# The first modulation's 128 uneven pieces in eight transfers instead of six

## The chip, the cores and the metric

One core of a Trainium2 chip. The metric is the device time of one execution in microseconds (us); a time given for a kernel is the median of its runs. Engines are named as the profile names them: PE is TensorE, DVE VectorE, ACT ScalarE, POOL GpSimd, SP SyncE. SP issues all loads of this kernel; the bytes are moved by the core's 16 DMA engines.

## What is computed

One transformer block for one token, with modulation from a condition vector and with attention over a cache of 8192 positions:

```python
mod = (silu(c) @ w_mod)              # 640 -> 6 x 640: sa, ca, ga, sb, cb, gb
h = layernorm(x) * (1 + ca) + sa
q = (h @ wq)                         # 32 heads of 192
p = softmax(q @ k_cache.T * 192**-0.5)   # per head, 8192 positions
x = x + ga * ((p @ v_cache) @ wo)
h = layernorm(x) * (1 + cb) + sb
x = x + gb * (relu(h @ w1 + b1)**2 @ w2 + b2)
```

All of it is in float32. The keys and values alone are 403 MB, read once.

## The kernel before, in words

All data in memory is laid out so that every load is a plain block of 128 rows. The loads go out on SP's one queue in the order of the program:

- `wm0_t` (L122): the first modulation's weights, the first query weights and the small vectors, 128 rows of 8514 floats.
- `wm0x` (L125): the rest of the first modulation. The last block of rows (`b == KB - 1` in `mod`) is split in a way of its own: 480 of its 1280 columns (`WX`) of each of the 128 rows are a *piece*, 1920 bytes. The 128 pieces are put into 64 rows of at most `SX = 7` pieces, as the table `XP` says: an entry `(a, k, n)` is one transfer of `k` rows, to rows `a`, `a+4`, ... of the tile, with `n` pieces side by side in a row. Pieces that no transfer fills stay at zero, set by two memsets (L120 on DVE for the first 3 pieces of a row, L121 on POOL for the other 4), and add nothing to the sum.
- `chunk0`, `chunk1`, ... (L240, in `load`): 53 blocks of keys, values, query weights and output weights, most of about 8 MB, in a ring of three buffers (`slot`); `wm0_t` lies in the same ring. After them come the loads of the second half (`wm1`, `w1`, `w2`, the last one in four parts).

On the other engines the program begins with `silu`, the product `mod(0, 2, ...)` (L198 for what is laid out evenly, L204 for the pieces: two matmuls for each of the 7 places of a row, whatever lies there), a layernorm, and the first query (L254). From then on DVE multiplies each chunk of keys by its query (L273) and sums (L281), PE sums up the values (L322), and the buffer is given back to `load(n + 3)`.

The framework gives each transfer a semaphore that counts its landing. It has eight for SP's queue (DMAHW0 to DMAHW7), handed out in turn, and a transfer that gets one that was used before is issued only after the transfer that used it has landed. A wait that SP stands at holds everything behind it on SP.

Of the kernel before, what the change touches and what calls it, by code (L numbers as in the profile page):

```python
# [38 lines left out]
EXTRA = {"o": WO, "q": WQ}  # L39
SLOT = 84 * DH  # L40
SX = 7
XP = ((32, 8, 5), (0, 3, SX), (1, 3, SX), (2, 3, SX), (3, 3, 6), (33, 1, SX))
WX = 3 * DG
W0 = KB * 2 * D - WX
VPC = 5
# [48 lines left out]
def block_kernel(ctx: ExitStack, tc: tile.TileContext, kv, wm0, wm0x, wm1, w1, w2, out):  # L94
# [28 lines left out]
    r = 0  # L123
    for a, k, n in XP:
        nc.sync.dma_start(wm0x_t[a:a + 4 * k:4, :n * WX], wm0x[r:r + k, :n * WX])  # L125
# [397 lines left out]
```

## Time and profile before

| | us |
|---|---|
| median of 3 runs | 1052.29 |
| lowest and highest | 1051.96, 1052.34 |
| the profiled execution: span from the first to the last instruction | 1050.0 |
| DVE busy | 826.1 |
| PE busy | 488.7 |

The profiled execution is told by its span; its own time on the device isn't given apart from that, and the median of the runs is 2.29 us over the span. The page gives the busy time of each engine, the DMA engines' busy share and rate in 40 slices, and the chain of work that ended last. The trace behind it can be asked for stretches: what each engine did in order of time, what SP issued and when, and how many bytes began to move in each slice of a stretch.

### The profile page before, as it was taken

The numbers are of one execution on the slowest core, as the hardware profiler recorded it, in microseconds if no ns is written. First come the engines' busy times: TensorE is split into PE (matmuls) and PEld (weight loads), VectorE is DVE, ScalarE is ACT, GpSimd is POOL, SyncE is SP. The second block draws the span as 40 slices with busy tenths as digits, with TensorE's granted clock in tenths as the row PEclk, the third lists the DMA queues.
The fourth block names the chain that finished last, engine by engine and source line by source line (L and its number), as shares of the span: only waits on it lengthen the run. The fifth ranks groups of instructions, "written<-read, shape, count | busy, mean of one in ns | idle before, by whom it ended". The sixth has DMA issues, their size and how long they took to land.

```text
span 1050.0 us, 5180 instructions
## 1 busy us (share of the span) xinstructions
PE 488.7 (47%) x2130; PEld 133.8 (13%) x2130; DVE 826.1 (79%) x405; ACT 44.9 (4%) x122; POOL 190.4 (18%) x61
## 2 busy tenths in 40 slices
PE   3253334455352363446354356345445346435287
PEld 1010001111010010101011011001011011001023
DVE  1799878876959969888697895999887977988812
ACT  0100000000000000000000000000000000000001
POOL 1113121121212211212121121122211211311200
PEclk9676576777685686668776576686777767768689
DMA  9999999999999999999999999999999999999998
GB/s 408 430 433 432 434 435 433 446 439 433 431 432 433 428 433 433 433 442 434 432 434 433 433 434 437 435 433 435 436 430 433 433 435 433 435 433 426 431 429 345
DMA packets 9144, 452.14 MB, mean 431 GB/s; under 512 B 1033, under 2 KB 1037, under 8 KB 1421
## 3 DMA queue, kind: packets, MB, share of 16 engines
q1 hardware_dynamic: 9118, 451.83, 99.5%
q8 instruction: 16, 0.26, 0.1%
q14 instruction: 6, 0.05, 0.0%
q10 hardware_dynamic: 4, 0.00, 0.0%
HBM read 451.82 MB, written 0.00 MB: 430 GB/s over the span
## 4 chain that ended last, share of the span: by engine, by line
DMA 53%; DVE 33%; PE 12%; ACT 1%; issue 0%; SPq 0%; DVEq 0%; ACTq 0%
DMA chunk<-in_kv 50%; DVE chunk L273 17%; DVE sc L281 13%; PE ps_o L322 6%; PE ps_q L254 2%; PE att_a L354 2%; DMA w_t<-in_w 2%; DMA wm_t<-in_wm 1%; DVE os L336 1%; DVE om L334 1%; PE ps_mx L297 1%; PE att_a L356 1%; ACT p L305 0%; PE ps_mod L198 0%; PE ps_mod L204 0%
## 5 line engine op out<-in xcount | busy, mean ns | idle before, releaser
L273 DVE TENSOR_TENSOR chunk<-chunk,qb 128x8064 f32<-128x8064 f32 (+19 forms) x81 | 419.6, 5211 | 127.3 <-DMA chunk<-in_kv 122.1
L281 DVE TENSOR_REDUCE sc<-chunk 128x25 f32<-128x4800 f32 (+21 forms) x109 | 333.8, 3096 | 0.4
L399 POOL TENSOR_TENSOR chunk<-chunk 128x1824 f32<-128x1824 f32 (+9 forms) x51 | 187.3, 3673 | 801.0 <-DVE chunk L273 568.6
L322 PE MATMUL ps_o<-chunk,p 128*32 128x512 f32 x1536 | 288.6, 719 | 70.1 <-DMA chunk<-in_kv 60.6
L297 PE MATMUL ps_mx<-ident,mp 128*128 128x128 f32 x32 | 14.6, 457 | 347.6 <-DVE mp L295 347.5
L322 PEld LDWEIGHTS ps_o<-chunk,p 128*32 128x32 f32 x1536 | 66.2, 129 | 268.1 <-issue 183.2
L354 PE MATMUL att_a<-chunk,oW 128*32 128x512 f32 x96 | 66.5, 850 | 45.0 <-ACT oW L352 45.0
L254 PE MATMUL ps_q<-chunk,ln_h 128*128 128x512 f32 x110 | 64.5, 746 | 25.2 <-DMA chunk<-in_kv 25.2
L297 PEld LDWEIGHTS ps_mx<-ident,mp 128*128 128x128 f32 x32 | 5.7, 177 | 376.3 <-DVE mp L295 308.2
L305 ACT ACTIVATE p<-sc,nm 128x256 f32<-128x256 f32 x32 | 16.2, 507 | 651.0 <-DVE nm L299 651.0
L254 PEld LDWEIGHTS ps_q<-chunk,ln_h 128*128 128x128 f32 x110 | 25.9, 246 | 61.6 <-issue 33.1
L334 DVE TENSOR_TENSOR om<-ps_o,mask 96x512 f32<-96x512 f32 x32 | 21.6, 675 | 8.9 <-PE ps_o L322 8.9
L299 DVE TENSOR_REDUCE nm<-ps_mx 128x1 f32<-128x128 f32 x32 | 9.3, 292 | 19.6 <-PE ps_mx L297 19.6
L354 PEld LDWEIGHTS att_a<-chunk,oW 128*32 128x32 f32 x96 | 12.4, 145 | 82.4 <-ACT oW L352 47.6
L336 DVE TENSOR_REDUCE os<-om 96x64 f32<-96x512 f32 x32 | 21.8, 682 | 1.1
L344 DVE TENSOR_REDUCE oT<-ps_oT 128x3 f32<-128x96 f32 x16 | 4.0, 248 | 18.4 <-PE ps_oT L340 18.4
L310 PE MATMUL ps_sum<-ident,wide 128*128 128x128 f32 x16 | 7.5, 467 | 22.4 <-ACT wide L308 22.4
L340 PE MATMUL ps_oT<-ident,os 96*128 96x96 f32 x16 | 4.9, 306 | 26.9 <-DVE os L336 26.9
L198 PE MATMUL ps_mod<-wm_t,silu 128*32 128x480 f32 (+2 forms) x78 | 9.1, 606 | 14.4 <-DVE silu L180 14.4
L356 PE MATMUL att_a<-chunk,oW 128*96 128x384 f32 x32 | 14.5, 536 | 0.0
L352 ACT ACTIVATE oW<-oT,r 128x96 f32<-128x96 f32 x16 | 5.9, 372 | 173.3 <-DVE oT L344 173.3
L255 ACT ACTIVATE qb<-ps_q 128x512 f32<-128x512 f32 x12 | 7.2, 597 | 130.6 <-PE ps_q L254 130.6
(79 smaller groups left out, 99.8 us busy)
## 6 DMA issues: line engine op xcount, KB each, us to landing
chunk<-in_kv SPq DMA_DIRECT2D x38, 8064.0 KB, 35.3
chunk<-in_kv SPq DMA_DIRECT2D x11, 8000.0 KB, 36.6
chunk<-in_kv SPq DMA_DIRECT2D x2, 7872.0 KB
chunk<-in_kv SPq DMA_DIRECT2D x1, 6144.0 KB, 22.8
wm_t<-in_wm SPq DMA_DIRECT2D x1, 4480.0 KB
wm_t<-in_wm SPq DMA_DIRECT2D x1, 4257.0 KB, 12.5
chunk<-in_kv SPq DMA_DIRECT2D x1, 3264.0 KB
chunk<-in_kv SPq DMA_DIRECT2D x1, 3072.0 KB
```

What stands on the lines that cost most here:

```text
L254: nc.tensor.matmul(ps, h1[:, b:b + 1].to_broadcast([P, P]), w[:, b], start=(b == 0), stop=(b == KB - 1))
L273: nc.vector.tensor_mul(pr, pr, q[:, None, :].to_broadcast([P, b - a, DH]))
L281: nc.vector.tensor_reduce(sc[:, a % SRING:a % SRING + b - a], src[:, a - first:b - first], axis=AX.X, op=ALU.add)
L297: nc.tensor.transpose(ps[:, :P], mp.to_broadcast([P, P]), ident)
L299: nc.vector.tensor_reduce(nm, ps[:, :P], axis=AX.X, op=ALU.max, negate=True)
L305: nc.scalar.activation(p, s[:, :, None].to_broadcast([P, NPOS, 32 // E]), AF.Exp, bias=nm, accum_out=sp[:, h % 2:h % 2 + 1])
L322: nc.tensor.matmul(ps_t[h][32 * g:32 * (g + 1)], p[:, E * j:E * (j + 1)].rearrange("p e r -> p (e r)"), t[:, g], start=(j == 0), stop=last)
L334: nc.vector.tensor_mul(om[:n], ps_t.pop(h)[:n].rearrange("p (d e) -> p d e", e=E), mask[:n, None, :].to_broadcast([n, ED, E]))
L336: nc.vector.tensor_reduce(os_[:n, h % 2], om[:n], axis=AX.X, op=ALU.add)
L354: nc.tensor.matmul(att_a[96:, :512], oW[:, j], w[:, j, :512], start=(first and j == 0), stop=(last and j == NV - 1))
L356: nc.tensor.matmul(att_a[:96, :NV * (D - 512)], oW.rearrange("p j r -> p (j r)"), w[:, :, 512:], start=first, stop=last)
L399: nc.gpsimd.tensor_add(half, half, kt[:, m:, DH // 2:])
```

## The change

Only the table `XP` differs. Before, 21 rows in 6 transfers carry 5, 7, 7, 7, 6 and 7 pieces a row; after, 32 rows in 8 transfers carry 2, 3, 4, 5, 7, 7, 4 and 2. Both carry the same 128 pieces, and the tile, the memsets and the matmuls are the same (the host fills `xp` and `xs` by the same table).

```diff
-XP = ((32, 8, 5), (0, 3, SX), (1, 3, SX), (2, 3, SX), (3, 3, 6), (33, 1, SX))
+XP = ((32, 7, 2), (33, 6, 3), (34, 5, 4), (35, 4, 5), (0, 3, SX), (1, 3, SX), (2, 3, 4), (3, 1, 2))
```

By row of a transfer, the pieces add up so: rows that stand first in their transfers carry 39 pieces before and 34 after; second and third rows 32 before and 32 after; the fourth to eighth 5 each before, and 14, 9, 5, 2 and 0 after.

SP's queue at the start of the program, before. `wm_t` is the tile of the first load and of the pieces, `chunk_100` and the following are chunk 0, 1, 2 and 3; in brackets stands what the issue waits for.

```order
L122 DMA wm_t<-in_wm 128x8514
L125 DMA wm_t<-in_wm0x 8x2400 [waits DVE_49,Pool_49]
L125 DMA wm_t<-in_wm0x 3x3360 x3
L125 DMA wm_t<-in_wm0x 3x2880
L125 DMA wm_t<-in_wm0x 1x3360
L240 DMA chunk_100<-in_kv 128x12288
L240 DMA chunk_102<-in_kv 128x16000 [waits DMAHW0_49]
```

And the same stretch after, where `chunk_102` and the following are chunk 0, 1 and 2:

```order
L122 DMA wm_t<-in_wm 128x8514
L125 DMA wm_t<-in_wm0x 7x960 [waits DVE_49]
L125 DMA wm_t<-in_wm0x 6x1440
L125 DMA wm_t<-in_wm0x 5x1920 [waits Pool_49]
L125 DMA wm_t<-in_wm0x 4x2400
L125 DMA wm_t<-in_wm0x 3x3360 x2
L125 DMA wm_t<-in_wm0x 3x1920
L125 DMA wm_t<-in_wm0x 1x960 [waits DMAHW0_49]
L240 DMA chunk_102<-in_kv 128x12288 [waits DMAHW1_49]
L240 DMA chunk_104<-in_kv 128x16000 [waits DMAHW2_49]
```

The first load uses DMAHW0. Before, the six transfers of pieces use 1 to 6, chunk 0 uses 7, and chunk 1 is the first that waits for a semaphore in use, that of the first load. After, the eighth transfer of pieces is the one that waits for the first load, and chunk 0 stands behind it and waits for the first transfer of pieces.

## Rows read from the trace of the kernel before

**Rows 1.** The page: span, engines, DMA in 40 slices, queues.
```profile
span 1050.0 us, 5180 instructions
PE 488.7 (47%) x2130; PEld 133.8 (13%) x2130; DVE 826.1 (79%) x405; ACT 44.9 (4%) x122; POOL 190.4 (18%) x61
...
DMA  9999999999999999999999999999999999999998
GB/s 408 430 433 432 434 435 433 446 439 433 431 432 433 428 433 433 433 442 434 432 434 433 433 434 437 435 433 435 436 430 433 433 435 433 435 433 426 431 429 345
...
q1 hardware_dynamic: 9118, 451.83, 99.5%
q8 instruction: 16, 0.26, 0.1%
```
**Rows 2.** Chain that ended last, program's end: start us, us, what.
```profile
1027.20 18.48 DMA w_t<-in_w
1045.72 0.75 PE ps_y L464 x16
1046.50 0.52 PE ps_y L464 x8
```
**Rows 3.** The same chain, program's beginning.
```profile
0.73 12.46 DMA wm_t<-in_wm
13.21 0.20 DVE small L129
...
19.05 3.90 PE ps_mod L204 x22
...
34.89 12.97 DVE chunk L273
```
**Rows 4.** SP in order of time: start us, us, engine, line, operation, tiles, count.
```profile
0.73 0.39 SPq L122 DMA_DIRECT2D wm_t<-in_wm  x1
3.28 4.11 SPq L125 DMA_DIRECT2D wm_t<-in_wm0x  x6
7.44 0.35 SPq L240 DMA_DIRECT2D chunk<-in_kv  x1
...
13.21 0.33 SPq L240 DMA_DIRECT2D chunk<-in_kv  x1
```
**Rows 5.** Line L125: issues on SP, ns min/median/max, first and last start.
```profile
L125 SPq DMA_DIRECT2D wm_t<-in_wm0x x6: 411/651/801, 3.3 to 7.0; - x6
```
**Rows 6.** What SP waited for from 0 to 60 us: us, times, longest.
```profile
SPq L240 <- DMA wm_t<-in_wm: 5.4, 1, 5.4
```
**Rows 7.** DMA issues, whole run: count, KB each, median us from issue to landing.
```profile
chunk<-in_kv SPq DMA_DIRECT2D x38, 8064.0 KB, 35.3
...
chunk<-in_kv SPq DMA_DIRECT2D x1, 6144.0 KB, 22.8
...
wm_t<-in_wm SPq DMA_DIRECT2D x1, 4257.0 KB, 12.5
```
**Rows 8.** DMA by slices of 62.5 ns, 0.5 to 3.0 us.
```profile
GB/s 0 0 0 0 0 0 0 0 0 0 0 0 0 0 0 0 0 0 0 2180 545 545 2724 1090 0 1090 545 0 0 0 0 0 0 0 0 0 0 0 0 0
```
**Rows 9.** The same, 12.0 to 14.5 us.
```profile
GB/s 0 0 0 0 0 307 0 461 1727 940 940 1573 1788 2575 786 786 215 0 0 0 215 215 0 0 215 0 0 0 215 215 0 0 215 0 0 0 0 1942 786 786
```
**Rows 10.** The same, 1047.5 to 1049.5 us (50 ns a slice), the output's transfers.
```profile
GB/s 0 0 0 0 0 0 0 0 0 0 0 0 0 0 0 0 0 0 0 0 26 0 26 0 0 0 0 0 0 0 0 0 0 0 0 0 0 0 0 0
```
**Rows 11.** SP in order of time, the output.
```profile
1047.76 0.28 SPq L470 DMA_DIRECT2D out_y<-y  x1
```
**Rows 12.** Stretches: us, busy us of PE, PEld, DVE, ACT, POOL, clock, DMA share, GB/s.
```profile
200.00:300.00 100.00, 45.94 (x181) 12.07 (x180) 81.84 (x38) 3.39 (x10) 17.97 (x5) 0.72 1.00 434
```
**Rows 13.** The same at the end.
```profile
1043.20:1043.60 0.40, 0.40 (x20) 0.34 (x12) 0.00 (x0) 0.00 (x0) 0.00 (x0) 1.00 0.75 308
...
1044.00:1045.00 1.00, 0.79 (x24) 0.68 (x24) 0.00 (x0) 0.00 (x0) 0.00 (x0) 1.00 0.76 315
1045.00:1045.60 0.60, 0.23 (x8) 0.00 (x0) 0.00 (x0) 0.00 (x0) 0.00 (x0) 1.00 0.73 291
1045.60:1046.00 0.40, 0.28 (x8) 0.27 (x12) 0.00 (x0) 0.00 (x0) 0.00 (x0) 1.00 0.51 198
1046.00:1046.50 0.50, 0.48 (x17) 0.15 (x8) 0.00 (x0) 0.00 (x0) 0.00 (x0) 1.00 0.00 0
```
**Rows 14.** DVE in order of time, with idle time before and its releaser.
```profile
59.19 6.15 DVE L273 TENSOR_TENSOR chunk<-chunk,qb 128x5760 f32<-128x5760 f32 x1
...
106.26 9.03 DVE L273 TENSOR_TENSOR chunk<-chunk,qb 128x1920 f32<-128x1920 f32 x2 [1.33 <-DMA chunk<-in_kv]
```

## The prediction

> **What bounds the kernel now.** I read the page first. The 16 DMA engines are 90% busy or more in every one of the 40 slices but the last, at 430 to 440 GB/s, while DVE is busy 79% and PE 47% of the span [rows 1]. So the loads are the bound: 452 MB at about 434 GB/s, the rate of the undisturbed middle [rows 12], are 1042 us of a span of 1050. Next the chain's two ends. At the end the chain is a load, three short products that wait for the last parts of it, and two DVE steps [rows 2]: whatever makes the last landing late makes the kernel late. At the beginning the chain is not on the loads: the first load lands at 13.19 (0.73 + 12.46), then come `silu`, the product, the layernorm and the first query, and DVE takes up chunk 0 only at 34.89 [rows 3]. Chunk 0 has landed by then (issued at 7.44, 22.8 us to landing: about 30.3) [rows 4, 7]. DVE first stands idle for a chunk just before 106.26 [rows 14]. In between it works off a lead that the loads have, and the DMA queue has a chunk or two in hand at all times (35.3 us from issue to landing [rows 7], against 8064 KB at 434 GB/s = 19.0 us). From 13 us to the end the loads thus run without a break, and a break anywhere is not made good later: the rate has no reserve.
>
> That is the question to put to this change: does it open a break in the loads, or does it only move pieces about?
>
> **The pieces.** A piece of 1920 bytes on one of 16 engines that share 434 GB/s (27.1 each) takes 71 ns. The slices after 13 us show single rows of 13.4 KB (215 GB/s in 62.5 ns) starting one after another about half a microsecond apart, while other engines begin the longer rows of chunk 0 [rows 9]. I read this as rows of one transfer going to different engines, and the first three rows of every transfer to the same three. So one engine has 39 pieces before (2.77 us), two have 32 (2.27), five have 5 (0.35), and eight have none. After, that is 34, 32, 32, then 14, 9, 5, 2, 0, and eight with none. Moving them costs no bytes: −0.35 us on the most loaded engine, +0.64 at worst on another. The two added issues on SP take 0.65 us each by the median of the six [rows 5]; the first seven fit between 3.28 and about 8.0, while the first load still moves until about 12.9. They are hidden. The memsets don't change, and the first transfer's shorter wait brings nothing, as DVE's memset is the later one.
>
> **The wait.** The eighth transfer of pieces has the semaphore of the first load, so SP holds it until that load has landed, and chunk 0 stands behind it on SP. Before, chunk 0 goes out at 7.44, and it is chunk 1 that waits there, 5.4 us, and goes out at 13.21, with chunk 0's bytes to cover it [rows 4, 6]. After, at 13.21 only the last small transfer goes out. I take 0.41 us for it: the shortest of the six, since the issues' times (3.28 to 7.39 in all, the last at 7.0) leave that for the one-row transfer [rows 4, 5]. With the gap of 0.05 that stands between the pieces and chunk 0 before, **chunk 0 goes out at 13.67, 6.23 us later**. Its own wait, for the first transfer of pieces, is over by then: that one's bytes are at the head of each engine's line behind the first load. The first load's bytes ran out at about 12.4 to 12.9: the engines begin the next rows there [rows 9]. From then until chunk 0's first bytes come, nothing but pieces is queued.
>
> How long is that break? The one load that starts from idle in this trace is the first: 12.46 us from issue to landing, of which 4257 KB (4.36 MB) at 434 GB/s are 10.04, so 2.42 us are lags at both ends [rows 3, 7]. Chunk 0 after would land at 13.67 + 2.42 + 14.50 (6144 KB at the same rate) = 30.59 on all engines. Before, on an engine without pieces, it follows the first load directly: 13.19 + 14.50 = 27.69. So those eight engines lose **2.90 us**. The five with 5 pieces would have landed 0.35 later anyway and lose **2.55**. Those with 32 pieces lose 0.63, the one with 39 about 0.1: their pieces fill the break. The low bound takes the lag as the output's transfers show it, 0.74 us or so from issue to the first byte (issued at 47.76, bytes from the slice at 48.50) [rows 10, 11]: 13.67 + 0.74 − 12.9 = **1.5 us**. Chunk 0 is a load from memory like the first, whose first bytes come 1.0 us after the issue and not before 1.75 [rows 4, 8], and whose first rows were slow as well, since no further row begins before 3.0; so I take it to be near the first load's lag. The high bound has 0.65 for the small issue and not 0.41: 3.14.
>
> [...]
>
> **Does the break reach the end?** Only if the engines that are last at the end are among those that lose. If only the three with 32 to 39 pieces were late, 13 of 16 would be idle in the last two microseconds. They are not: from 1043.2 to 1045.6 the DMA share is 0.73 to 0.76, which is 12 of 16 engines [rows 13]. So besides the three, nine others are as late at the end, which had 5 pieces or none. The page shows something that falls on single engines: 16 instruction fetches of 16 KB on a queue of their own (0.26 MB) [rows 1]. I take it that an engine which serves one moves nothing else meanwhile. Whatever made the nine late, they were 2.3 us ahead at chunk 0 and are not at the end, and 2.5 to 2.9 us more at the beginning are 2.5 to 2.9 more at the end. As the rows don't say whether one with 5 pieces or with none is the very last, I take the middle, **+2.7 us**. Nothing hides it: the compute at the beginning has 34.89 − 30.59 = 4.3 us left for chunk 0, and later chunks come later for DVE, which waits for them anyway from 106 us on. The pieces themselves are needed at 19.05 [rows 3]; the last would land at about 13.2 + 2.27 + 0.14, well before.
>
> **Sum.** On the profiled execution: 1050.0 + 2.7 = 1052.7. The median of the runs stands 2.29 over that span, so 1052.29 + 2.7 = **1055.0 us**, 0.26% slower.
>
> **Rivals.**
>
> *The loaded engines cover it (not slower).* The end is set by the engines with 39 and 32 pieces, which lie 2.3 to 2.8 us behind the others from the first chunk on. Then the break is spent where the others wait in any case, and what counts is 5 pieces fewer on the most loaded engine less the little it loses: −0.35 to +0.63, 1051.9 to 1052.9. It decides if at most three engines are at work in the last 2 us before the last landing. For it speaks that before the change these engines are the last at chunk 0 by the sum above; against it the 12 of 16. Chance 0.11. [...]
>
> *The break isn't there.* SP's wait ends earlier than I take it to, or the engines hold enough work: the time stays, 1052.3. For it would speak a chunk 0 that is issued before 13.2, and nothing in the order or in the 5.4 us that chunk 1 waits does. Chance 0.03.
>
> *One engine more in the way.* The wait for two more transfers adds instructions on PE and SP; if this brings one more fetch of 16 KB on an engine that is among the last, it loses what a fetch costs, 16 KB at 27.1 GB/s = 0.6 us and, if it has to wait its turn behind a row of 64 KB, up to some 2.4 more: 1055.6 to 1058. Chance 0.06.
>
> **How the numbers follow.** The forecast has 0.80. Its own range is 1052.29 + 1.5 to 1052.29 + 3.14, 1053.8 to 1055.4. I give 1053.8 to 1055.7, since the last rival begins there. Of 0.2% as the least that a measurement of this kernel can tell from no change, the bound is 1054.4, a break of 2.1 us; the low part of the forecast's range is under it, for which I set 0.10 of the 0.80. So slower is 0.70 + 0.06 = 0.76; same is 0.10 + 0.11 + 0.03 = 0.24, of which I give 0.01 to faster, for no case reaches 1050.2.
>
> **What would show it.** In the profile after: SP issues seven transfers of pieces by about 8.0, one at 13.2, and chunk 0 at about 13.7, with the wait for the first load in front of L125 and no longer in front of L240; between 13 and 14.7 us the DMA share falls to three to five engines of 16, with hardly any bytes beginning, and then 16 rows of 48 KB begin within half a microsecond; chunk 0 is about 17 us from issue to landing, not 22.8; the last landing comes 2.7 us later, and the steps behind it are unchanged. The prediction is wrong if chunk 0 goes out before 13, or if the last landing moves by under 2 us though the gap is there: then the late engines at the end are those that had the pieces, or the start from idle is faster than the first load's.

## The result and the profile after

| | before | after |
|---|---|---|
| median of 6 runs, us | 1052.12 (1051.96 to 1052.34) | 1055.34 (1054.80 to 1055.55) |
| profiled execution, span, us | 1050.0 | 1053.0 |

The ratio is 1.003, with a 95% interval of 1.002 to 1.004: the changed kernel is slower by 3.2 us. Forecast were 2.7 us and 1055.0.

The page, where it answers to [rows 1]: the busy times of the engines are nearly as before (PE 6.4 us more), the bytes too. Only the first of the 40 slices moves clearly fewer, 367 GB/s and not 408.

```profile
span 1053.0 us, 5182 instructions
PE 495.1 (47%) x2130; PEld 134.8 (13%) x2130; DVE 826.2 (78%) x405; ACT 44.9 (4%) x122; POOL 190.4 (18%) x61
...
GB/s 367 434 434 431 429 437 439 435 435 434 432 435 434 427 431 437 434 440 433 433 427 434 434 440 433 429 434 436 439 434 432 429 434 439 431 434 424 430 430 339
...
q8 instruction: 17, 0.28, 0.1%
```

SP in order of time after, from 8 to 14 us (start us, us, what; it answers to [rows 4]), and what SP waited for in the first 60 us (it answers to [rows 6]):

```profile
7.77 5.65 SPq L125 DMA_DIRECT2D wm_t<-in_wm0x  x2
13.47 0.82 SPq L240 DMA_DIRECT2D chunk<-in_kv  x2
...
SPq L125 <- DMA wm_t<-in_wm: 4.7, 1, 4.7
```

The seventh transfer of pieces starts at 7.77, the eighth ends at 13.42, and chunk 0 goes out at 13.47, where it was 7.44. The wait for the first load, in front of L240 before, stands in front of L125 now.

The stretch from 13.0 to 14.4 us in the kernel before and after (us, busy us of PE, PEld, DVE, ACT, POOL, clock, DMA share, GB/s begun):

```profile
13.00:14.40 1.40, 0.03 (x4) 0.03 (x5) 0.76 (x4) 0.21 (x1) 0.00 (x0) 1.00 0.36 154
```
```profile
13.00:14.40 1.40, 0.10 (x4) 0.10 (x8) 0.76 (x4) 0.21 (x1) 0.00 (x0) 1.00 0.23 96
```

This table books a row where it begins, so the first line doesn't mean idle engines: before, 13 engines were in the middle of a row of chunk 0 that had begun by 13.0 [rows 9]. After, nothing but pieces begins here, at a share of 0.23, 3.7 engines of 16, where the prediction has three to five. The slices show it better. The bytes that begin to move, in slices of 100 ns, are in the kernel before from 12 to 16 us, and in the changed one from 14 to 18 us:

```profile
GB/s 0 0 0 192 288 1079 1175 1966 1744 983 134 0 0 269 0 134 0 0 269 0 134 0 0 1214 983 1590 1966 1966 0 134 0 0 0 0 492 0 0 0 0 0
```
```profile
GB/s 134 0 0 134 2043 2534 492 530 77 0 0 983 492 492 0 0 0 0 0 0 0 0 0 492 0 0 0 492 0 492 492 2458 492 492 0 492 0 1475 0 492
```

A row of chunk 0 is 49 KB, 492 GB/s in one slice. Before, the first rows begin at 12.5 to 12.9 (what begins at 12.4 are pieces) and the second ones at 14.3 to 14.7: a row takes 1.8 us. After, 15 first rows begin at 14.4 to 15.3 and the 16th at 16.3; the second rows begin at 16.8 to 17.9. So there are two losses: the rows begin some 2 us later, and an engine's first row takes mostly 2.2 to 3.3 us where it took 1.8.

At the program's end the chain is as before [rows 2], with the last wait 3.12 us later (1049.62 against 1046.50):

```profile
1030.68 18.11 DMA w_t<-in_w
1048.84 0.75 PE ps_y L464 x16
1049.62 0.52 PE ps_y L464 x8
```

### The profile page after: what moved, and what is told of

It reads as the page before. It is cut to its first block, busy times and chain, and to the rows that moved or that the text cites. A ratio compares the mean times of both kernels' runs of the same rounds, so it can differ in the third digit from the quotient of the medians.

```text
span 1053.0 us, 5182 instructions
## 1 busy us (share of the span) xinstructions
PE 495.1 (47%) x2130; PEld 134.8 (13%) x2130; DVE 826.2 (78%) x405; ACT 44.9 (4%) x122; POOL 190.4 (18%) x61
## 4 chain that ended last, share of the span: by engine, by line
DMA 56%; DVE 30%; PE 13%; ACT 1%; issue 0%; SPq 0%; DVEq 0%; ACTq 0%
DMA chunk<-in_kv 53%; DVE chunk L273 16%; DVE sc L281 12%; PE ps_o L322 6%; PE ps_q L254 2%; PE att_a L354 2%; DMA w_t<-in_w 2%; DMA wm_t<-in_wm 1%; DVE os L336 1%; DVE om L334 1%; PE att_a L356 0%; PE ps_mod L198 0%; ACT p L305 0%; PE ps_mx L297 0%; PE ps_mod L204 0%
## 5 line engine op out<-in xcount | busy, mean ns | idle before, releaser
L297 PE MATMUL ps_mx<-ident,mp 128*128 128x128 f32 x32 | 14.5, 452 | 348.0 <-DVE mp L295 348.0
L354 PE MATMUL att_a<-chunk,oW 128*32 128x512 f32 x96 | 69.2, 880 | 44.9 <-ACT oW L352 44.9
L354 PEld LDWEIGHTS att_a<-chunk,oW 128*32 128x32 f32 x96 | 12.5, 146 | 82.4 <-ACT oW L352 47.6
L198 PE MATMUL ps_mod<-wm_t,silu 128*32 128x480 f32 (+2 forms) x78 | 9.3, 619 | 14.3 <-DVE silu L180 14.3
```

What stands on the lines that cost most here:

```text
L198: nc.tensor.matmul(ps[32 * g:32 * (g + 1), at], e[:, b:b + 1].to_broadcast([P, 32]), wg, start=(b == 0), stop=(b == KB - 1 and (wx is None ...
L297: nc.tensor.transpose(ps[:, :P], mp.to_broadcast([P, P]), ident)
L354: nc.tensor.matmul(att_a[96:, :512], oW[:, j], w[:, j, :512], start=(first and j == 0), stop=(last and j == NV - 1))
```

## The experiments

The theory: the loss is the time that chunk 0 is issued too late to follow the first load without a break. Its rivals: the pieces' new places on the engines; the number of transfers; the one instruction fetch more that the page shows (17 and not 16). Each time stands beside that of the kernel before on the same chip, 1051.98 to 1052.12.

| kernel | chunk 0 goes out, us | median, us | ratio to before, 95% interval |
|---|---|---|---|
| before | 7.44 | 1052.0 | |
| `pool2`: the changed table, chunk 0 not held | 7.76 | 1052.5 | 1.0005 (0.9996 to 1.0014) |
| `six_even`: six transfers, other places | 7.70 | 1052.1 | 1.0002 (0.9993 to 1.001) |
| `d9`: chunk 0 held by POOL | 9.01 | 1051.97 | 1.0 (0.9991 to 1.0009) |
| `d10`: the same, longer | 10.01 | 1053.45 | 1.0012 (1.0002 to 1.0021) |
| `d12`: the same, longer still | 11.76 | 1053.47 | 1.0012 (1.0004 to 1.0021) |
| `seven`: old places, seven transfers | 13.34 | 1055.07 | 1.0029 (1.0017 to 1.004) |
| after: eight transfers | 13.47 | 1055.34 | 1.003 (1.002 to 1.004) |
| `ten`: old places, ten transfers | 14.43 | 1056.37 | 1.0041 (1.0027 to 1.0055) |
| `filled`: as `seven`, 983 KB more | 13.19 | 1056.15 | 1.0039 (1.0026 to 1.0051) |
| `filled2`: as `seven`, 1966 KB more | 13.27 | 1056.39 | 1.004 (1.0028 to 1.0053) |

### The changed table without the wait

```diff
-    for a, k, n in XP:
-        nc.sync.dma_start(wm0x_t[a:a + 4 * k:4, :n * WX], wm0x[r:r + k, :n * WX])
+    for i, (a, k, n) in enumerate(XP):
+        queue = nc.sync if i < 6 else nc.gpsimd
+        queue.dma_start(wm0x_t[a:a + 4 * k:4, :n * WX], wm0x[r:r + k, :n * WX])
```

> The changed table as it is, eight transfers with 34, 32, 32, 14, 9, 5 and 2 pieces on the engines, but the last two are issued from POOL's queue, which has semaphores of its own. SP then has the first load, six transfers of pieces and chunk 0 on eight semaphores, and chunk 0 waits for nothing. If the break before chunk 0 is the whole loss, the time is that of the kernel before, 1052.1 us within 0.4, and chunk 0 is issued by about 8 us. If the pieces' new places or the number of transfers cost something, it stays near 1055.3 or at least over 1053.

It took 1052.5 us, not to be told from the kernel before. SP's rows:

```profile
3.22 4.50 SPq L126 DMA_DIRECT2D wm_t<-in_wm0x  x6
7.76 6.33 SPq L241 DMA_DIRECT2D chunk<-in_kv  x2
```

With the same eight transfers and the same places of the pieces, 2.8 of the 3.2 us are gone once chunk 0 goes out at 7.76. Of the remaining 0.5 the interval doesn't exclude zero.

### The wait with the old table

```diff
-XP = ((32, 8, 5), (0, 3, SX), (1, 3, SX), (2, 3, SX), (3, 3, 6), (33, 1, SX))
+XP = ((32, 8, 5), (0, 3, SX), (1, 3, SX), (2, 3, SX), (3, 3, 6), (33, 1, 4), (34, 1, 3))
```

> The kernel before with its old places for the pieces (39, 32, 32, 5 on five), only the one-row transfer of 7 pieces is cut into two one-row transfers of 4 and 3 pieces. That makes seven transfers, and chunk 0 is the one that has the first load's semaphore. If the wait is the cause, chunk 0 goes out at 13.15 us, 0.3 before the changed kernel's 13.47, and the time is 1052.1 + 2.9 = 1055.0 (0.3 under the changed kernel's 1055.3). If the places of the pieces or one fetch more made the loss, 1052.1 to 1052.5: engines and bytes are as before, and 13 KB more or less on no engine.

```diff
-XP = ((32, 8, 5), (0, 3, SX), (1, 3, SX), (2, 3, SX), (3, 3, 6), (33, 1, SX))
+XP = ((32, 8, 5), (0, 3, SX), (1, 3, SX), (2, 3, SX), (3, 3, 3), (12, 3, 3), (33, 1, 4), (34, 1, 1), (35, 1, 1), (37, 1, 1))
```

> As the last, but ten transfers: the fifth and sixth of the kernel before are cut into 3 and 3 pieces a row and into 4, 1, 1 and 1 pieces. The eighth to tenth and chunk 0 each wait for an earlier transfer, chunk 0 for the third one of pieces, which lands at about 14.4 us. If the loss follows the time at which chunk 0 goes out, that is 14.4 to 14.5, 0.95 after the changed kernel, and the time is 1055.3 + 0.95 = 1056.3. If the loss comes once, with the eighth semaphore, and not by the length of the wait, it is 1055.0 to 1055.4.

SP's row for chunk 0 with seven transfers, and the fetches on its page:

```profile
13.34 0.82 SPq L240 DMA_DIRECT2D chunk<-in_kv  x2
...
q8 instruction: 16, 0.26, 0.1%
```

And with ten:

```profile
7.67 6.63 SPq L125 DMA_DIRECT2D wm_t<-in_wm0x  x4
14.43 0.35 SPq L240 DMA_DIRECT2D chunk<-in_kv  x1
```

Cutting one transfer of 13 KB in two costs 3.0 us, with the old places and with 16 fetches as before. So neither the places nor the fetch is needed for the loss. With ten transfers chunk 0 goes out 1.09 us later than with seven, and the time is 1.30 us longer: the loss goes on with the length of the wait. Both came out within 0.1 us of what was expected.

### Places alone

```diff
-XP = ((32, 8, 5), (0, 3, SX), (1, 3, SX), (2, 3, SX), (3, 3, 6), (33, 1, SX))
+XP = ((32, 5, 5), (0, 4, SX), (1, 3, SX), (2, 3, SX), (3, 3, SX), (33, 3, 4))
```

> The kernel before with its number of transfers, six, and the pieces on other places: rows of 5, 7, 7, 7, 7 and 4 pieces in transfers of 5, 4, 3, 3, 3 and 3 rows, which is 37, 37, 37, 12 and 5 pieces by row of a transfer in place of 39, 32, 32 and five times 5. Chunk 0 goes out as before, at about 7.4. If only the wait counts, moving pieces by up to 7 (0.5 us) between engines is worth nothing that shows: 1052.0 to 1052.5. If the places are what the changed kernel lost by, 1053 or more.

Chunk 0 goes out at 7.70, and the time is 1052.1 us, as before. Half a microsecond of bytes more or less on single engines doesn't show.

### Is it idle time of the engines?

```diff
+FILL = 1920
...
         nc.sync.dma_start(wm0x_t[a:a + 4 * k:4, :n * WX], wm0x[r:r + k, :n * WX])
         r += k
+    nc.sync.dma_start(wm0_t[:, W0 + WQ + 96:W0 + WQ + 96 + FILL], wm0[:, :FILL])
```

> The kernel before with one more transfer behind its six of pieces: 128 rows of 1920 floats (983 KB, 2.27 us at 434 GB/s) into a part of the buffer that nothing reads. It takes the eighth semaphore, so that chunk 0 waits for the first load as in the kernel with seven transfers, but the engines have 2.27 us of rows to move meanwhile. If the loss is time in which engines have nothing to move, the added bytes cost nothing beside the kernel with seven transfers: 1052.1 + 2.27 + a rest of 0 to 0.6 = 1054.4 to 1055.0. If the loss is something else, the bytes come on top: 1055.0 + 2.27 = 1057.3.

Chunk 0 goes out as late as in `seven`:

```profile
13.19 0.80 SPq L242 DMA_DIRECT2D chunk<-in_kv  x2
```

It took 1056.15, between the two: 1.1 us over `seven` where the bytes take 2.27. So 1.2 us of the bytes were free, and 1.85 us of loss are left over them. The stretch in which the other kernels' engines idle is full here:

```profile
13.00:14.40 1.40, 0.05 (x4) 0.05 (x8) 0.76 (x4) 0.21 (x1) 0.00 (x0) 1.00 0.99 416
```

So what is lost here isn't lost in this stretch. The slices of this kernel from 14 to 18 us say where:

```profile
GB/s 288 384 461 269 499 576 307 154 933 722 645 492 1628 0 77 154 492 1060 154 492 568 154 77 0 154 568 0 154 77 77 77 77 492 492 77 492 1475 1966 0 0
```

Chunk 0's first rows (the large entries) begin between 14.8 and 15.3 on seven engines and at 15.7 to 16.5 on others, and the second ones, the large entries at the end, at 17.5 to 17.7: a first row mostly takes 2.5 us or more here too, not 1.8. Chunk 0 was issued at 13.19, about 1.9 us before the filling ended on most of the engines (12.8 + 2.27 = 15.1; in the trace it ends between 14.8 and 15.35 on the thirteen without a long line of pieces). Seven of them go on to chunk 0 within 0.15 us, and their first rows are slow all the same; the six that begin at 15.7 or later stand idle for some 0.4 us to more than one before. A row's time can be read where it begins alone in a narrow stretch, as its share times 16 times the stretch. Below, the first line is the kernel before at 12.5 us: 5.70 x 16 x 0.02 = 1.82 us. The others are `filled`: 2.87 at 14.8, 2.38 at 16.57, and 2.18 at 17.28, on an engine with a long line of pieces, 4.1 us after the issue:

```profile
12.50:12.52 0.02, 0.00 (x0) 0.00 (x0) 0.00 (x0) 0.00 (x0) 0.00 (x0) 1.00 5.70 2458
```
```profile
14.80:14.82 0.02, 0.02 (x4) 0.00 (x0) 0.00 (x0) 0.00 (x0) 0.00 (x0) 1.00 8.97 2458
16.57:16.58 0.01, 0.01 (x8) 0.01 (x4) 0.00 (x0) 0.00 (x0) 0.00 (x0) 1.00 14.86 4915
17.28:17.30 0.02, 0.02 (x4) 0.00 (x0) 0.00 (x0) 0.00 (x0) 0.00 (x0) 1.00 6.82 2458
```

At the end of the program three engines and then one at most are at work, for 1.4 us:

```profile
1049.00:1049.90 0.90, 0.39 (x16) 0.07 (x10) 0.00 (x0) 0.00 (x0) 0.00 (x0) 1.00 0.20 80
1049.90:1050.40 0.50, 0.50 (x16) 0.36 (x16) 0.00 (x0) 0.00 (x0) 0.00 (x0) 1.00 0.04 15
```

That gave the theory its second form: **chunk 0 has to be issued some time ahead of the moment its rows are needed, and where it wasn't, its first rows began late or took longer (2.2 to 3.3 us after the change, mostly 2.5 or more in `filled`, 1.8 before), whether or not the engine was idle**. Why a first row takes longer then, no run here shows. Drawn back at one us per us, `seven`, after and `ten` put that lead at 2.3 us. By that alone `filled`, with 1.9, should have lost 0.4 and not 1.85; that one us per us doesn't hold, the runs with a held chunk 0 show too, below.

With twice the filling (`FILL = 3840`) chunk 0 has the lead although it goes out just as late:

> As the kernel with 983 KB of filling, but with twice as much: 3840 floats a row, 1966 KB, 4.53 us at 434 GB/s, in the same place before chunk 0. Chunk 0 still goes out at about 13.2, but the engines have rows until about 17.4 and get chunk 0's rows some 3 us before they need them. If the loss is a matter of how long chunk 0 is issued ahead of its need, nothing is left of it and the added bytes alone count: 1052.0 + 4.53 = 1056.6, within 0.5. If holding chunk 0 costs the 1.85 us that the smaller filling left over its own bytes whatever is in front of it, 1052.0 + 4.53 + 1.85 = 1058.4.

```profile
13.27 0.82 SPq L242 DMA_DIRECT2D chunk<-in_kv  x2
```

1056.39, which is 4.37 over the kernel before for bytes that take 4.53: nothing of the loss is left. The slices from 16 to 20 us show the first rows at 16.9 to 17.6 and the second ones at 18.8 to 19.4, 1.8 us apart as in the kernel before:

```profile
GB/s 461 154 154 307 922 768 154 154 307 952 1628 1290 492 492 983 1137 645 154 0 0 154 0 307 0 0 0 154 492 1290 1475 492 492 1137 1475 983 0 0 492 0 0
```

### How much lead

Here the pieces are those of the kernel before, and POOL writes zeros into the buffer of chunk 0, which chunk 0 then overwrites; chunk 0 waits for that.

```diff
+HOLD = 8200
...
             chunk_t[n] = slot(f"chunk{n}")
+            if n == 0:
+                nc.gpsimd.memset(chunk_t[n][:, :HOLD], 0.0)
```

> The kernel before with its six transfers of pieces, but POOL writes zeros into 8200 columns of chunk 0's buffer first, and chunk 0 waits for that: it goes out at about 10.1 us and not at 7.44. If a load must be issued some 2.3 us ahead of the moment its rows are needed (12.5 to 12.9), as the runs with seven, eight and ten transfers give it when their loss is drawn back to nothing at one us for each us (13.34 - 3.04 = 10.3), there is no loss yet: 1052.0 to 1052.3. If every delay on SP costs, 2.7 us: 1054.7.

> As the last with 10300 columns: chunk 0 goes out at about 11.85. By the lead of 2.3 us it loses 11.85 - 10.3 = 1.5 us: 1053.5. If the engines only need the issue 1.0 us ahead, the time from the first load's issue to its first bytes, it is within that (11.85 + 1.0 = 12.85) and loses nothing: 1052.0 to 1052.3.

Chunk 0's issue with the shorter hold and with the longer one:

```profile
10.01 3.64 SPq L243 DMA_DIRECT2D chunk<-in_kv  x2
```
```profile
11.76 1.78 SPq L243 DMA_DIRECT2D chunk<-in_kv  x2
```

The longer one (`HOLD = 10300`) came out where the lead of 2.3 us puts it, 1.45 us slower, and against the rival by which an issue 1.0 us ahead is enough. The shorter one was a miss: 1.4 us slower, where no loss was expected. As 1.75 us more of delay cost nothing between the two, the longer one's hit is no proof of one us per us. The slices of the shorter one from 12.0 to 14.5 us (62.5 ns each):

```profile
GB/s 0 0 0 0 0 0 154 307 307 1727 940 154 1573 1788 2360 1002 786 215 0 0 0 215 0 1002 0 215 0 0 0 215 0 215 0 215 0 0 0 184 0 184
```

Chunk 0's rows begin as in the kernel before, up to 13.0, and then one more begins at 13.44 (1002 GB/s is a row of 49 KB and one of 13 KB). One engine got its first row late:

```profile
13.43:13.45 0.02, 0.00 (x0) 0.00 (x0) 0.02 (x1) 0.00 (x0) 0.00 (x0) 1.00 11.89 3130
```

The stretch in which it begins holds 3.80 us of rows (11.89 x 16 x 0.02); less 0.50 for the 13 KB row, its first row took 3.3 us where 1.8 is usual, so that it was some 2 us behind. At the other end of the same execution one engine alone is at work for more than a microsecond, a DMA share of 0.05 to 0.06 being one of 16:

```profile
1046.60:1047.20 0.60, 0.51 (x16) 0.18 (x8) 0.00 (x0) 0.00 (x0) 0.00 (x0) 1.00 0.06 26
1047.20:1048.20 1.00, 0.52 (x16) 0.42 (x16) 0.00 (x0) 0.00 (x0) 0.00 (x0) 1.00 0.05 20
```

By the trace it is the same one: followed from load to load by its rows, an engine that is 2.2 us behind falls back by 1.4 at each of two instruction fetches and is last at the end. In the kernel before, none of the three engines that begin 2.2 to 2.9 us late serves a fetch of 16 KB (more on this below). In the longer hold all thirteen engines without a long line of pieces are 1.3 to 1.9 us late when chunk 0 ends, and none by more, which is another way to the same time.

So 2.3 us is a lead for most of the engines, not for the slowest. One microsecond more:

> As the kernel with 8200 columns of zeros, with 7000: chunk 0 goes out at about 9.0 us, 1.0 earlier. There it lost 1.4 us although its rows came without a break on nearly all engines, and at the end of its profile one engine alone is at work for the last 1.5 us. If that engine began late because 2.5 us of lead are too few for the slowest engine, 3.5 us should be enough: 1052.0 to 1052.4. If the zeros on POOL or any wait in front of chunk 0 cost that, it stays near 1053.4.

```profile
9.01 4.45 SPq L243 DMA_DIRECT2D chunk<-in_kv  x2
```

1051.97 us: no loss, with the same wait and nearly the same zeros. With these loads in front, the lead that is enough for all engines lies between 2.5 us (chunk 0 out at 10.0 for rows needed from 12.5 on) and 3.5 us (out at 9.0). It is no constant: in `filled` a row that began 3.4 us after the issue still took 2.38 us, and one 4.1 us after it 2.18.

## Why the prediction was right

**What bounds it.** That the loads have no reserve, so that a break at 13 us is still there at the end, held: the second rows of chunk 0 begin 2.5 to 3.2 us later, the last wait ends 3.12 later, and the time is 3.2 longer. DVE, with its lead at the beginning, took no harm; it waits for the first time at 88.81 (1.25 us), one chunk earlier than in [rows 14].

```profile
88.81 8.96 DVE L273 TENSOR_TENSOR chunk<-chunk,qb 128x8448 f32<-128x8448 f32 x1 [1.25 <-DMA chunk<-in_kv]
```

**The pieces.** Costed at nothing, and `six_even` and `pool2` bear that out within 0.1 and 0.5 us.

**The wait.** It is the cause: `pool2` takes it away, `seven` has it alone. The issue of chunk 0 was put at 13.67 and was at 13.47, since the first load landed at 13.11 (0.73 + 12.38) in this execution and the issue of the small transfer took 0.28 and not 0.41.

**The size of the break** is the term that was too small. 2.7 us stood in the sum; 3.2 were measured, 3.4 if the earlier issue is counted. The working took the lag of the first load, 2.42 us between its issue and its landing over its bytes, and the middle between engines with 5 pieces and with none. As a mean over the engines that held: put at 30.59 on all engines, 30.39 with the earlier issue, chunk 0's rows end between 29.6 and 30.6 on fifteen engines in this trace and at 31.5 on one. But it isn't one lag. Rows begin 1.0 us after the issue (13.47 to 14.4) as in the first load (0.73 to 1.72), a first row took 2.2 to 3.3 us on most engines in place of 1.8, and one engine's began a microsecond after all others. What counts are the engines that are last at the end, and they were among those with the longer lags (below). The low bound of 1.5 us, a break that ends with the first byte, left the slow first rows out altogether; in `filled` seven engines have next to no break before theirs.

Two small readings of the prediction are off and change nothing: the slices between the first and the last move 426 to 446 GB/s and not 430 to 440, and the first load's bytes begin in the slice from 1.69 to 1.75 us, not after 1.75 [rows 1, 8].

**Who is last at the end.** Twelve engines were late in [rows 13], which pass over 0.4 us with a share of 0.83 (13 engines); by the rows' own times twelve engines end at 1045.6 to 1046.1, so the reading holds. After, it is that of ten or eleven engines until 1048.0, of six or seven then, and of one or two at the last:

```profile
1046.50:1048.00 1.50, 1.14 (x36) 0.73 (x28) 0.00 (x0) 0.00 (x0) 0.00 (x0) 1.00 0.66 273
1048.00:1048.70 0.70, 0.26 (x8) 0.00 (x0) 0.00 (x0) 0.00 (x0) 0.00 (x0) 1.00 0.41 161
1048.70:1049.60 0.90, 0.75 (x16) 0.42 (x16) 0.00 (x0) 0.00 (x0) 0.00 (x0) 1.00 0.08 31
```

The end is thus more ragged than before, and the very last engines are late by some tenths more than the 2.7 us of the sum. The rival by which the three loaded engines cover the break fell with that: `seven` has their old load and loses 3.0.

Why nine others were late the prediction left open, with the fetches as a guess. The trace bears the guess out, if one follows each engine's rows by their starts and durations and compares the engines at the end of every load. Before the first fetch thirteen engines of the kernel before lie within 0.5 us, and three, with the long lines of pieces, 2.2 to 2.9 behind the first. At the fetch of 16 KB at 62.9 us one engine falls from 0.3 to 1.7 us behind: no row begins on it in the 0.87 us from 62.87 to 63.74, and the next takes 2.93 us where 2.38 is usual. The fetch lasts 0.89 us, and the prediction took one at 0.6. At the later ones an engine falls back each time by about 1.4. At 1009.6 us, after 14 fetches, ten engines, those three among them, lie 2.6 to 3.0 behind. No run was made without the fetches. Counted in the same way from the first engine of the kernel before, the last two of the changed kernel are 6.2 behind at 1012.4 us, which is 3.2 us more than before: they were 3.4 behind at the end of chunk 0, neither the first nor the last there, and each had two fetches since. The engine whose first row began at 16.3 had been 4.5 behind, had no fetch, and is not the last.

**One fetch more** did come (17), with a chance of 0.06, but not where that rival has it. Up to 1049.7 us, when the last wait for a load is over (1049.62), the changed kernel has had 16 as well, and the 17th follows at 1049.8:

```profile
q8 instruction: 16, 0.26, 0.1%
```

So it isn't what the change lost by, and `seven` loses 3.0 us with 16. The 0.3 us between `seven` and the changed kernel aren't clear of the spread of their runs.

## What to carry to other kernels

Where loads bound a kernel, count the transfers that are in flight before a large load and the semaphores that the framework has for their queue: here one small transfer too many put chunk 0 behind the first load's landing (out at 13.34 in `seven` and not at 7.44), and nothing of the 3.0 us was made good later. What mattered here was not only whether the engines ran dry but how far ahead the next load was issued: 3.5 us were enough for all 16 engines, 2.5 us left one behind, and a filling transfer of 4.5 us in between did as well as an earlier issue, one of 2.3 us did not. Look for the slowest single engine at the end, in the DMA share in sixteenths, before an average rate is trusted.

## What the runs showed that was not expected

- Chunk 0's first rows took longer where it was issued just before they were needed: 1.8 us for 49 KB with the issue 5 us ahead (before), mostly 2.2 to 3.3 us where the first byte came 1.0 us after the issue (after), and mostly 2.5 us or more with 1.9 us of lead behind other rows (`filled`).
- Moving 983 KB more in the break cost 1.1 us; moving 1966 KB more cost 1.3 us. The second 983 KB took 0.2 us: with them the first rows take 1.8 us again.
- The engines differed in how much lead they needed: at 2.5 us (`d10`) one of the engines without a long line of pieces began chunk 0 half a microsecond after the others and took 3.3 us for its first row, and the kernel ended 1.4 us later.
- In the trace of the kernel before, an engine falls back by about 1.4 us at each instruction fetch of 16 KB and doesn't make it good. In the changed kernel the two engines that are last at 1012.4 us were 3.4 us behind after chunk 0 and had served two fetches each.
